# The first loads of x and wk as halves from two queues, k's first products by blocks, and one warm-up less

## The chip, the cores and the metric

The kernel runs on one core of one Trainium2 chip. The metric is the device time of one execution in microseconds (us). The kernel before takes 182.62 us, the median of 3 runs (182.56 to 182.65).

## What is computed

Two linear-attention blocks A and B work on the same input x (2048 rows, 640 columns, bf16), each with weights of its own, and a gate mixes their outputs row by row. Cut to what matters:

```python
def block(x, wqkv, wo):                      # x: 2048 x 640, 32 heads of 20
    q, k, v = split_heads(x @ wqkv)
    phi = lambda t: where(t > 0, t + 1, exp(t)) + 1e-6
    pq, pk = phi(q), phi(k)
    kv = einsum("hsd,hse->hde", pk, v)
    z = pk.sum(over s)
    o = einsum("hqd,hde->hqe", pq, kv) / (einsum("hqd,hd->hq", pq, z) + 1e-6)
    return merge_heads(o) @ wo

g = sigmoid((x * gate_w).sum(-1))            # one number for a row
out = g * block(x, A_wqkv, A_wo) + (1 - g) * block(x, B_wqkv, B_wo)
```

## The kernel before

x is cut into 16 chunks of 128 rows (`ST`), its 640 columns into 5 blocks of 128 (`DT`), and a row of k into two halves of 320 (`HF`, `hf` 0 and 1). TensorE (PE) contracts over partitions, so it needs x with its columns on the partitions: the tile xT. The tile xn holds x as it lies in memory. wk, wq and wv are the thirds of wqkv, each as 5 blocks of 128 rows.

The stages are: k of block A for all chunks, with q of A between them (to about 49 us); sums over the rows for A; then k, q and sums for B; then the outputs. The change touches only the start, up to the end of k of chunks 0 and 1, and the queue of loads behind it.

DMAs are issued by two engines, SP (`nc.sync`) and ACT (`nc.scalar`). Each issues its DMAs in the order of the code, and one that must wait holds up all behind it on that engine. A DMA reports its end on a semaphore. These are the first DMAs before the change:

- lines 127 and 128: chunk 0 of x from SP, chunk 1 from ACT, whole rows of 1280 bytes;
- lines 129 to 132: the five blocks of wk in turn from SP, ACT, SP, ACT, SP; the row of gate weights (`grow`, in the tile R) from ACT between ACT's two;
- lines 133 and 134: chunks 2 and 3 of x from SP by transposing DMAs, straight into xT;
- lines 136 and 137: wq in three pieces (blocks 0 and 1, 2 and 3, 4) from SP;
- lines 138 and 139: the other three quarters of xT by transposing DMAs from SP.

Meanwhile PE runs warm-ups (lines 164 and 165): products of ones with ones, six of 512 columns and one of 256, into a bank that is overwritten later. Then comes `k_first` (lines 234 to 269), whose order is written out by hand (`manual_schedule`, line 719). `turn(i)` transposes chunk i on PE, block by block (line 239). `keep(i, lo, hi)` lets VectorE (DVE) copy blocks lo to hi of it to xT (line 243). `part(cs, hfs, chunks)` issues the k products of the named blocks, halves and chunks (line 218). `gate_column` turns the gate's row on PE (line 169) and copies it into an extra column of wk (line 170), so that the second half of each k product (321 columns) also gives the gate's logit; every product of that half waits for it. `k_done` (line 223) is phi of the finished chunk: exp on ACT, the rest on DVE. Then `k_first` does chunks 2 and 3 (line 269) with xT from the transposing DMAs, and q of the first quarter follows (lines 291 and 301).

Before the change the order on PE is: turn 0, turn 1; block 0 and 1 of chunk 0 (first halves); block 0 of chunk 1; the gate's row; block 1 of chunk 1; block 2 of chunk 0; second halves of blocks 0 and 1 of chunk 0; and so on to block 2; then blocks 3 and 4 of chunk 0, of chunk 1. DVE copies blocks 0 and 1 of chunk 0, then of chunk 1, then blocks 2 to 4 of chunk 0, the gate's column, blocks 2 to 4 of chunk 1.

Of the kernel before, what the change touches and what calls it, by code (L numbers as in the profile page):

```python
# [8 lines left out]
P = 128  # L9
# [5 lines left out]
S, D, H = 2048, 640, 32  # L15
Dh = D // H
DT = D // P
ST = S // P
NB = 4
CB = 4  # L20
HB = 512
HF = D // 2
# [10 lines left out]
def kernel(  # L33
# [11 lines left out]
    nc = tc.nc  # L45
    x2 = A_x.flatten_outer_dims()
# [24 lines left out]
    xn = persist.tile([P, ST, D], BF16, name="xn")  # L71
# [34 lines left out]
    wq_dram = [A_wqkv.rearrange("(c p) f -> p c f", p=P), B_wqkv.rearrange("(c p) f -> p c f", p=P)]  # L106
# [6 lines left out]
    wk = [None, None]  # L113
    wv = [None, None]
    wq = [None, None]
    wk[0] = wpool.tile([P, DT, D + 16], BF16, tag="wk", name="wkA")
    def load_x(eng, i):
        eng.dma_start(out=xn[:, i, :], in_=x2[i * P:(i + 1) * P, :])

    def x_turned(lo, hi):  # L120
        nc.sync.dma_start_transpose(out=xT[:, :, lo:hi], in_=x2[lo:hi, :])

    def load_wk(eng, lo, hi):
        eng.dma_start(out=wk[0][:, lo:hi, 0:D], in_=wq_dram[0][:, lo:hi, D:2 * D])

    grow = R[0][0:DT, 0:P]
    load_x(nc.sync, 0)
    load_x(nc.scalar, 1)
    for c, eng in enumerate((nc.sync, nc.scalar, nc.sync, nc.scalar, nc.sync)):
        load_wk(eng, c, c + 1)  # L130
        if c == 1:
            nc.scalar.dma_start(out=grow, in_=gate_w.rearrange("(c p) -> c p", p=P))
    for i in (2, 3):
        x_turned(i * P, (i + 1) * P)
    wq[0] = wpool.tile([P, DT, D], BF16, tag="wq", name="wqA")
    for lo, hi in ((0, 2), (2, 4), (4, DT)):
        nc.sync.dma_start(out=wq[0][:, lo:hi, :], in_=wq_dram[0][:, lo:hi, 0:D])
    for n in range(1, NB):
        x_turned(n * HB, (n + 1) * HB)


    make_identity(nc, ident[:])
    for r in range(2):
        nc.gpsimd.memset(maskE[r][:], 1.0)
        for sign, base in ((1, 0), (-1, Dh - 1)):
            nc.gpsimd.affine_select(
                out=maskE[r][:], in_=maskE[r][:], pattern=[[-sign * Dh, WT[0] // Dh], [0, Dh]],
# [4 lines left out]
    for sign, base in ((1, 0), (-1, TW - 1)):  # L152
        nc.gpsimd.affine_select(
            out=headE[:], in_=headE[:], pattern=[[-sign * TW, H]],
# [6 lines left out]
    turned = [ps_raw("xt", i) for i in range(2)]  # L161
    warm = turned[1].bitcast(FP32).rearrange("p (b n) -> p b n", b=2)
    one_l, one_r = [nc.const_aps.tensor(1.0, [P, n], BF16) for n in (P, HB)]
    for n in (HB,) * 6 + (HB // 2,):
        nc.tensor.matmul(warm[:, 1, 0:n], lhsT=one_l, rhs=one_r[:, 0:n], start=True, stop=True)  # L165

    def gate_column(gcol):

        nc.tensor.transpose(out=gcol, in_=grow, identity=ident[0:DT, 0:DT])
        nc.vector.tensor_copy(out=wk[0][:, :, D:D + 1], in_=gcol.rearrange("p (c n) -> p c n", n=1))  # L170
# [45 lines left out]
    def k_mm(b, i, c, pt, hf):  # L216
        w = HF + (hf if b == 0 else 0)
        nc.tensor.matmul(  # L218
            pt[:, hf, 0:w], lhsT=xT[:, c, i * P:(i + 1) * P], rhs=wk[b][:, c, hf * HF:hf * HF + w],
            start=(c == 0), stop=(c == DT - 1),  # L220
        )

    def k_done(b, i, pt, lifted=False):
        side = (lambda: nc.scalar.copy(out=logit[:, i:i + 1], in_=pt[:, 1, HF:HF + 1])) if b == 0 else None
        phi(pk[:, i, :].rearrange("p (b n) -> p b n", b=2), pt[:, :, 0:HF], HF, lifted, side)

    def k_chunk(b, i, slot=None, lifted=False):
        pt = ps(f"k{'AB'[b]}", slot)
        for hf in range(2):
            for c in range(DT):  # L230
                k_mm(b, i, c, pt, hf)
        k_done(b, i, pt, lifted)

    def k_first():

        def turn(i):
            for c in range(DT):
                cols = slice(c * P, (c + 1) * P)
                nc.tensor.transpose(out=turned[i][:, cols], in_=xn[:, i, cols], identity=ident[:])

        def keep(i, lo, hi):
            src = turned[i][:, 0:D].rearrange("p (c n) -> p c n", c=DT)
            nc.vector.tensor_copy(out=xT[:, lo:hi, i * P:(i + 1) * P], in_=src[:, lo:hi])  # L243

        def part(cs, hfs, chunks=(0, 1)):
            for c in cs:
                for hf in hfs:
                    for i in chunks:
                        k_mm(0, i, c, pts[i], hf)

        for i in range(2):
            turn(i)
            keep(i, 0, 2)
        part((0, 1), (0,), (0,))
        part((0,), (0,), (1,))
        keep(0, 2, DT)
        gate_column(turned[1][:, 2 * HB:2 * HB + DT])
        keep(1, 2, DT)
        part((1,), (0,), (1,))
        part((2,), (0,), (0,))  # L260
        part((0, 1), (1,), (0,))
        part((2,), (0,), (1,))
        part((0, 1), (1,), (1,))
        part((2,), (1,))
        for i in range(2):
            part((3, 4), (0, 1), (i,))
            k_done(0, i, pts[i])
        for i in range(2, CB):
            k_chunk(0, i, i - 2)
# [278 lines left out]
    part = [slice(n * RB, (n + 1) * RB) for n in range(4)]  # L548
# [170 lines left out]
    with tc.manual_schedule():  # L719
        k_first()  # L720
# [19 lines left out]
    with tc.manual_schedule():  # L740
# [100 lines left out]
        for i in range(half - 1):  # L841
            p, after = pairs[i:i + 2]
# [48 lines left out]
```

## Time and profile before

| | before |
|---|---|
| median of 3 runs | 182.62 us (182.56 to 182.65) |
| the profiled execution's own time | 182.69 us |
| its span, first to last instruction | 180.9 us |
| PE busy | 177.1 us (98%), 1340 matmuls |
| DVE busy | 147.5 us (81%) |
| ACT busy | 85.8 us (47%) |
| granted clock of TensorE | 1.00 |

The profile is that of one execution. Its times count from the first instruction of the span. "PE" are matmuls, "PEld" the weight loads ahead of them, "SPq" and "ACTq" the DMA issues of SP and ACT. A matmul's recorded length holds its way through the array, so the pace of a row of matmuls is read from their starts. "Landing" is the time from a DMA's issue to its end; a row has one only where the trace could tell it. Behind `<-` in square brackets stands what ended the engine's idle time.

### The profile page before, as it was taken

The numbers are of one execution on the slowest core, as the hardware profiler recorded it, in microseconds if no ns is written. First come the engines' busy times: TensorE is split into PE (matmuls) and PEld (weight loads), VectorE is DVE, ScalarE is ACT, GpSimd is POOL, SyncE is SP. The second block draws the span as 40 slices with busy tenths as digits, with TensorE's granted clock in tenths as the row PEclk, the third lists the DMA queues.
The fourth block names the chain that finished last, engine by engine and source line by source line (L and its number), as shares of the span: only waits on it lengthen the run. The fifth ranks groups of instructions, "written<-read, shape, count | busy, mean of one in ns | idle before, by whom it ended". The sixth has DMA issues, their size and how long they took to land.

```text
span 180.9 us, 3414 instructions
## 1 busy us (share of the span) xinstructions
PE 177.1 (98%) x1340; PEld 119.3 (66%) x1345; DVE 147.5 (81%) x247; ACT 85.8 (47%) x140; POOL 5.4 (3%) x18
## 2 busy tenths in 40 slices
PE   8999999999999999999999999999999999999993
PEld 4566657765577777777775555677777777677772
DVE  0386868989998896888778999969999799977863
ACT  2245846889971101378784779921101863111010
POOL 6000000000000000000000000000003200000000
PEclk9999999999999999999999999999999999999999
DMA  5999999523100216431116000000325451133323
GB/s 179 209 269 173 244 370 284 112 49 134 58 0 6 70 47 209 110 108 36 57 34 190 19 0 0 0 4 14 125 78 132 137 181 50 36 109 112 109 92 127
DMA packets 22842, 19.33 MB, mean 107 GB/s; under 512 B 10538, under 2 KB 22058, under 8 KB 22826
## 3 DMA queue, kind: packets, MB, share of 16 engines
q1 hardware_dynamic: 20744, 16.95, 34.0%
q10 hardware_dynamic: 2082, 2.17, 3.6%
q8 instruction: 10, 0.16, 0.4%
q14 instruction: 6, 0.05, 0.1%
HBM read 12.29 MB, written 4.53 MB: 93 GB/s over the span
## 4 chain that ended last, share of the span: by engine, by line
PE 97%; issue 0%; DVE 0%
PE gs L370 17%; PE kA L218 12%; PE ox L590 12%; PE kB L218 12%; PE qB L281 12%; PE qA L281 6%; PE oz L590 6%; PE qA L291 5%; PE gB L329 2%; PE gA L329 2%; PE ow L590 2%; PE xt L165 2%; PE qA L301 1%; PE mA L494 1%; PE s L494 1%; PE oy L590 1%
## 5 line engine op out<-in xcount | busy, mean ns | idle before, releaser
L218 PEld LDWEIGHTS <-xT 128*128 128x128 bf16 x320 | 31.0, 98 | 12.8 <-DVE xT L243 0.2
L210 DVE TENSOR_SCALAR e<-e 128x640 bf16<-128x640 bf16 (+2 forms) x53 | 18.9, 357 | 7.3 <-ACT e L205 6.7
L218 PE MATMUL kB<-wkB,xT 128*128 128x320 bf16 x160 | 23.1, 299 | 0.0
L218 PE MATMUL kA<-wkA,xT 128*128 128x320 bf16 (+1 forms) x160 | 22.9, 301 | 0.0
L281 PE MATMUL qB<-xT,wqB 128*128 128x512 bf16 x98 | 21.6, 379 | 0.1
L205 ACT ACTIVATE e<-kB 128x640 bf16<-128x640 f32 x16 | 11.2, 703 | 15.8 <-DMA wqB<-in_B_wqkv_dram 9.4
L281 PEld LDWEIGHTS <-wqB 128*128 128x128 bf16 x100 | 11.7, 117 | 9.7
L205 ACT ACTIVATE e<-kA 128x640 bf16<-128x640 f32 x16 | 11.2, 704 | 8.3 <-PE kA L218 8.3
L205 ACT ACTIVATE e<-qA 128x1024 bf16<-128x1024 f32 (+1 forms) x11 | 10.4, 946 | 6.4 <-PE qA L291 5.1
L648 ACT COPY u<-ox 128x320 f32<-128x320 f32 x8 | 3.4, 425 | 20.6 <-PE ox L590 20.6
L205 ACT ACTIVATE e<-qB 128x1024 bf16<-128x1024 f32 x10 | 10.2, 1023 | 5.6 <-PE qB L281 4.9
L370 PEld LDWEIGHTS <-xn 128*128 128x128 bf16 x96 | 9.2, 98 | 3.9 <-issue 0.4
L370 PEld LDWEIGHTS <-S 128*128 128x128 bf16 x96 | 9.4, 98 | 3.6
L281 PE MATMUL qA<-xT,wqA 128*128 128x512 bf16 x49 | 10.9, 379 | 0.1
L214 DVE SCALAR_TENSOR_TENSOR pk<-kB,e 128x640 bf16<-128x640 f32 x12 | 9.9, 824 | 1.2
L590 PEld LDWEIGHTS <-xT 128*128 128x128 bf16 x85 | 8.1, 98 | 2.9
L590 PEld LDWEIGHTS <-pqTB 128*128 128x128 bf16 x80 | 7.8, 98 | 3.3 <-issue 0.2
L590 PEld LDWEIGHTS <-pqTA 128*128 128x128 bf16 x80 | 7.7, 98 | 2.9
L370 PE MATMUL gs<-pk,xn 128*128 128x320 bf16 x64 | 9.5, 299 | 0.0
L281 PEld LDWEIGHTS <-wqA 128*128 128x128 bf16 x50 | 5.9, 117 | 4.8
L291 PE MATMUL qA<-xT,wqA 128*128 128x512 bf16 x38 | 8.9, 379 | 0.1
L212 DVE TENSOR_TENSOR pk<-pk,e 128x640 bf16<-128x640 bf16 x12 | 5.9, 492 | 2.8 <-ACT pk L209 2.2
(123 smaller groups left out, 296.9 us busy)
## 6 DMA issues: line engine op xcount, KB each, us to landing
xn<-in_A_x_dram SPq DMA_DIRECT2D x1, 2240.0 KB, 10.0
out_dram<-pk SPq DMA_DIRECT2D x14, 160.0 KB, 1.8
wvA<-in_A_wqkv_dram SPq DMA_DIRECT2D x1, 800.0 KB
wkB<-in_B_wqkv_dram SPq DMA_DIRECT2D x1, 800.0 KB, 4.7
wqB<-in_B_wqkv_dram ACTq DMA_DIRECT2D x1, 800.0 KB, 6.5
wvB<-in_B_wqkv_dram SPq DMA_DIRECT2D x1, 800.0 KB
MA<-mA_dram SPq DMA_DIRECT2D x1, 800.0 KB, 6.1
MB<-mB_dram SPq DMA_DIRECT2D x1, 800.0 KB
```

The costliest lines, as they stand in the source:

```text
L165: nc.tensor.matmul(warm[:, 1, 0:n], lhsT=one_l, rhs=one_r[:, 0:n], start=True, stop=True)
L205: nc.scalar.activation(out=e[:], in_=src, func=ACT.Exp)
L210: nc.vector.tensor_scalar(e[:], e[:], 1.0, EPS, op0=ALU.min, op1=ALU.add)
L212: nc.vector.tensor_tensor(out=dst, in0=dst, in1=e[:], op=ALU.max)
L214: nc.vector.scalar_tensor_tensor(out=dst, in0=src, scalar=1.0 + EPS, in1=e[:], op0=ALU.add, op1=ALU.max)
L218: nc.tensor.matmul(pt[:, hf, 0:w], lhsT=xT[:, c, i * P:(i + 1) * P], rhs=wk[b][:, c, hf * HF:hf * HF + w], start=(c == 0), stop=(c == DT - 1),
L281: nc.tensor.matmul(pt[:, u, :], lhsT=mixed(wq[b][:, c, :], m), rhs=xT[:, c, n * HB:(n + 1) * HB], start=(c == 0), stop=(c == DT - 1),)
L291: nc.tensor.matmul(pt[:, u, :], lhsT=mixed(wq[b][:, c, :], m + u), rhs=xT[:, c, n * HB:(n + 1) * HB], start=(c == 0), stop=(c == DT - 1),)
L329: nc.tensor.matmul(pt[:, hf, 0:HF], lhsT=xn[:, i, c * P:(c + 1) * P], rhs=pk[:, i, hf * HF:(hf + 1) * HF], start=(i == 0), stop=(i == ST - 1),
L370: nc.tensor.matmul(pt[:, n, 0:HF], lhsT=left[:, i, n * P:(n + 1) * P], rhs=right[:, i, :], start=(first and i == 0), stop=(i == hc - 1), s ...
L494: nc.tensor.matmul(dst[:w, 0:HF], lhsT=KVA[:rows, k, 0:w], rhs=wo_sb[b][:rows, k, n * HF:(n + 1) * HF], start=True, stop=True,)
L590: nc.tensor.matmul(dst, lhsT=left[:, c, r0:r0 + P], rhs=right[:, c, :], start=(first and c == 0), stop=(c == DT - 1), skip_group_check=not ...
```

## The change

- Chunks 0 and 1 of x and block 0 of wk come one after the other, each as two DMAs: its first 320 columns from SP, its last 320 from ACT.
- Then SP issues block 1 of wk and ACT the gate's row, ACT block 2, and SP blocks 3 and 4 in one DMA.
- wq comes in two pieces (blocks 0 to 2, blocks 3 and 4) instead of three, and the last two quarters of xT in one transposing DMA instead of two. The number of DMAs ahead of xn's rest stays 16.
- One of the six warm-ups of 512 columns is left out.
- DVE copies all of chunk 0 before chunk 1's first blocks, and the k products go by blocks: block 0 of both chunks, the gate's row, block 1 of both chunks, the second halves of blocks 0 and 1, then block 2.

```diff
-    def load_x(eng, i):
-        eng.dma_start(out=xn[:, i, :], in_=x2[i * P:(i + 1) * P, :])
+    sides = [(nc.sync, slice(0, HF)), (nc.scalar, slice(HF, D))]
+
+    def load_x(i):
+        for eng, cols in sides:
+            eng.dma_start(out=xn[:, i, cols], in_=x2[i * P:(i + 1) * P, cols])
...
-    load_x(nc.sync, 0)
-    load_x(nc.scalar, 1)
-    for c, eng in enumerate((nc.sync, nc.scalar, nc.sync, nc.scalar, nc.sync)):
-        load_wk(eng, c, c + 1)
-        if c == 1:
-            nc.scalar.dma_start(out=grow, in_=gate_w.rearrange("(c p) -> c p", p=P))
+    for i in range(2):
+        load_x(i)
+    for eng, cols in sides:
+        eng.dma_start(out=wk[0][:, 0, cols], in_=wq_dram[0][:, 0, D + cols.start:D + cols.stop])
+    load_wk(nc.sync, 1, 2)
+    nc.scalar.dma_start(out=grow, in_=gate_w.rearrange("(c p) -> c p", p=P))
+    load_wk(nc.scalar, 2, 3)
+    load_wk(nc.sync, 3, DT)
     for i in (2, 3):
         x_turned(i * P, (i + 1) * P)
     wq[0] = wpool.tile([P, DT, D], BF16, tag="wq", name="wqA")
-    for lo, hi in ((0, 2), (2, 4), (4, DT)):
+    for lo, hi in ((0, 3), (3, DT)):
         nc.sync.dma_start(out=wq[0][:, lo:hi, :], in_=wq_dram[0][:, lo:hi, 0:D])
-    for n in range(1, NB):
-        x_turned(n * HB, (n + 1) * HB)
+    for lo, hi in ((1, 2), (2, NB)):
+        x_turned(lo * HB, hi * HB)
...
-    for n in (HB,) * 6 + (HB // 2,):
+    for n in (HB,) * 5 + (HB // 2,):
...
         for i in range(2):
             turn(i)
             keep(i, 0, 2)
-        part((0, 1), (0,), (0,))
-        part((0,), (0,), (1,))
-        keep(0, 2, DT)
+            if i == 0:
+                keep(0, 2, DT)
+        part((0,), (0,))
         gate_column(turned[1][:, 2 * HB:2 * HB + DT])
         keep(1, 2, DT)
-        part((1,), (0,), (1,))
-        part((2,), (0,), (0,))
-        part((0, 1), (1,), (0,))
-        part((2,), (0,), (1,))
-        part((0, 1), (1,), (1,))
-        part((2,), (1,))
+        part((1,), (0,))
+        part((0, 1), (1,))
+        part((2,), (0, 1))
         for i in range(2):
             part((3, 4), (0, 1), (i,))
             k_done(0, i, pts[i])
```

## The prediction

> **What bounds the kernel now.** I read the page's shares first, then its chain.
>
> ```profile
> PE 177.1 (98%) x1340; PEld 119.3 (66%) x1345; DVE 147.5 (81%) x247; ACT 85.8 (47%) x140; POOL 5.4 (3%) x18
> PE 97%; issue 0%; DVE 0%
> ```
>
> PE works for 177.1 of 180.9 us and is 97% of the chain that ended last. So time can only be won where PE idles, or where it does work that nobody needs. All the edits lie in the first loads and in k's first products, so next comes the chain's first stretch, in order of time (start, length, what).
>
> ```profile
> 0.83 2.93 PE xt L165 x7
> 3.77 1.07 PE xt L239 x10
> ...
> 4.86 0.80 PE kA L218 x3
> ...
> 5.77 5.31 PE kA L218 x37
> ```
>
> The reader is to see two things. First, 2.93 us of L165 are the warm-ups, filler that runs until x is there. Second, TensorE is slow at first: three k products take 0.80 us (0.27 each), the next 37 take 5.31 (0.14 each, with a wait among them). The timeline of the head has the warm-ups too at the slow pace, 0.43 for 512 columns (2.50 and 2.92), which at 0.14 for 320 would be 0.22:
>
> ```profile
> 0.79 0.41 ACTq L118 DMA_DIRECT2D xn<-in_A_x_dram  x1
> 0.80 0.39 SPq L118 DMA_DIRECT2D xn<-in_A_x_dram  x1
> 1.23 0.46 ACTq L124 DMA_DIRECT2D wkA<-in_A_wqkv_dram  x1
> 1.25 1.37 SPq L124 DMA_DIRECT2D wkA<-in_A_wqkv_dram  x3
> 1.72 0.58 ACTq L132 DMA_DIRECT2D R<-in_gate_w_dram  x1
> 2.33 0.36 ACTq L124 DMA_DIRECT2D wkA<-in_A_wqkv_dram  x1
> 2.50 0.15 PEld L165 LDWEIGHTS <-const-bfloat16-1.0 128*128 128x128 bf16 x1 [0.28 <-issue]
> 2.73 1.28 ACT L205 ACT_TABLE_LOAD   x1 [2.73 <-issue]
> 2.92 0.15 PEld L165 LDWEIGHTS <-const-bfloat16-1.0 128*128 128x128 bf16 x1 [0.28 <-issue]
> 3.58 0.98 PEld L239 LDWEIGHTS <-xn 128*128 128x128 bf16 x10 [0.51 <-DMA xn<-in_A_x_dram]
> 3.59 1.25 PE L239 MATMUL xt<-ident,xn 128*128 128x128 bf16 x10
> 3.73 2.64 SPq L121 DMA_TRANSPOSE xT<-in_A_x_dram  x2
> 4.34 0.29 DVE L243 COPY xT<-xt 128x256 bf16<-128x256 bf16 x1 [3.37 <-PE xt L239]
> 4.87 0.55 DVE L243 COPY xT<-xt 128x256 bf16<-128x256 bf16 x2 [0.24 <-PE xt L239]
> ...
> 6.41 1.60 SPq L137 DMA_DIRECT2D wqA<-in_A_wqkv_dram  x3
> ```
>
> So full speed comes at about 5.4, some 4.5 us after the first matmul at 0.83. The turning of x starts at 3.59, where the last warm-up (half of one, from 3.35) ends and where x chunk 0 has just landed: warm-ups and x end together. Five instants of narrow timelines close the head: the first product of chunk 1, the last one of block 2, the first ones of block 3 and of chunk 2, and q's first.
>
> ```profile
> 5.35 0.31 PE L218 MATMUL kA<-wkA,xT 128*128 128x320 bf16 x1
> 6.86 0.30 PE L218 MATMUL kA<-wkA,xT 128*128 128x321 bf16 x1
> 7.10 0.43 PE L218 MATMUL kA<-wkA,xT 128*128 128x320 bf16 x2
> 8.19 0.43 PE L218 MATMUL kA<-wkA,xT 128*128 128x320 bf16 x2
> 10.91 0.38 PE L291 MATMUL qA<-xT,wqA 128*128 128x512 bf16 x1
> ```
>
> From 8.19 on PE runs without a gap worth counting, so **the change is worth what it moves the start of chunk 2, 8.19**, as long as later loads keep up.
>
> **The change part by part.**
>
> *One warm-up less.* It takes one interval, 2.92 - 2.50 = 0.42 to 0.43 us: filler ends at 3.16 instead of 3.59. This is a gain only if x is there; if not, PE idles instead and nothing is won.
>
> *x in halves, one chunk after the other.* Landings (the last number, median us from the issue) come from the DMA view, rates from windows, whose last column is GB/s:
>
> ```profile
> wqA<-in_A_wqkv_dram SPq DMA_DIRECT2D x2, 320.0 KB, 3.6
> wkA<-in_A_wqkv_dram SPq DMA_DIRECT2D x3, 160.0 KB, 3.6
> wkA<-in_A_wqkv_dram ACTq DMA_DIRECT2D x2, 160.0 KB, 3.8
> xn<-in_A_x_dram ACTq DMA_DIRECT2D x1, 160.0 KB, 2.9
> ...
> xT<-in_A_x_dram SPq DMA_TRANSPOSE x3, 3.9
> ```
>
> ```profile
> 1.50:1.75 0.25, 0.25 (x2) 0.11 (x1) 0.00 (x0) 0.00 (x0) 0.25 (x1) 1.00 0.00 0
> 1.75:2.64 0.89, 0.89 (x4) 0.33 (x3) 0.00 (x0) 0.00 (x0) 0.85 (x6) 1.00 0.78 184
> 1.75:3.08 1.33, 1.33 (x5) 0.48 (x4) 0.00 (x0) 0.35 (x1) 1.29 (x8) 1.00 0.86 247
> 1.75:3.53 1.78, 1.78 (x6) 0.48 (x4) 0.00 (x0) 0.81 (x1) 1.62 (x9) 1.00 0.92 278
> ```
>
> A chunk of x is 164 kB. 0.89 x 184 = 164 kB are moved by 2.64, 1.33 x 247 = 328 kB (both chunks) by 3.08, 1.78 x 278 = 495 kB (and one block of wk) by 3.53. Chunk 1, issued at 0.79, landed at 0.79 + 2.9 = 3.69, which is 0.61 after the bytes for both were through. Today chunk 0 shares the engines with chunk 1; after the change its halves have them alone, so chunk 0 should land near 2.64 + 0.61 = 3.25. Rows of 640 bytes cost more per byte. The queue rows of two windows (2.75 to 3.5 with 1280-byte reads; 177.55 to 177.95 with mostly 640-byte stores) price them:
>
> ```profile
> DMA packets 252, 0.28 MB, mean 374 GB/s; under 512 B 33, under 2 KB 252, under 8 KB 252
> ...
> q1 hardware_dynamic: 146, 0.17, 65.7%
> q10 hardware_dynamic: 106, 0.12, 42.5%
> ```
>
> ```profile
> q10 hardware_dynamic: 137, 0.08, 62.1%
> ```
>
> 252 packets took 108.2% of 16 x 0.75 us, 51.5 ns each; 137 took 62.1% of 16 x 0.40, 29 ns each. Two halves are 58 against 51.5, or 12%: 0.1 us on 0.89. I take 3.35 for chunk 0 (bounds: 3.16, where the filler ends and nothing earlier helps, and 3.69, where chunk 1 lands today). [...]
>
> The transposes go by columns of 128, and the first two need the left half alone, so only the third (0.21 later) waits for the right half. The chain then behaves as if turning began at about 3.20 (bounds 3.16 and 3.55).
>
> *Products by blocks.* Today the first product of chunk 1 comes 5.35 - 3.59 = 1.76 after the first transpose: five transposes, DVE's copy of chunk 0, five transposes, DVE's copy of chunk 1. The new order puts the copy of chunk 0's last three blocks ahead of chunk 1's first copy; DVE idles 0.24 there now (4.63 to 4.87), and the copy is about 0.3, so I charge nothing (bounds: -0.03 and +0.1). That product comes at 3.20 + 1.76 = 4.96. Its wk block, as two halves, is third in line: 3.53 + 0.61 plus 0.2 for small rows, 4.35, before the first product at about 4.45 (the row's 3.6 from 1.25 is 4.85 today).
>
> From there to chunk 2 takes 2.84 today, which holds 0.11 of waiting for block 3 (6.86 + 0.136 = 6.99, it starts at 7.10). The new order has one product more behind this point (18, not 17; +0.14), does not wait there (-0.11), and runs about 0.08 of it at half speed, since full speed comes at 5.4 and does not move with x. 4.96 + 2.84 + 0.14 - 0.11 + 0.08 = 7.91, against 8.19: **-0.28 us**.
>
> *What is issued later.* The transposing DMA at 3.73 writes a part of xT that nothing has touched, and still the queue's waits say:
>
> ```profile
> SPq L121 <- DMA xn<-in_A_x_dram: 1.1, 1, 1.1
> ```
>
> It is the ninth DMA, it leaves when chunk 1 has landed (3.69), so eight may be under way, and the ninth waits for the first. After the change eight DMAs are x (four), wk block 0 (two), block 1 and the gate's row. **The ninth and tenth are wk block 2 and blocks 3 to 4.** Today these leave by about 2.6 (L124's rows); then they leave when chunk 0's halves have landed, about 3.35. First bytes follow an issue by 1.0 us (issue 0.80, nothing moves before 1.75), so at 4.35; the engines are then just done with block 1 (3.53 + 164 kB at 374 GB/s + 0.2 for small rows = 4.2). 492 kB at 374 GB/s are 1.3 us: through at 5.7, landed at 6.3 by the lag of 0.61. By the wk rows (3.6 to 3.8 from the issue) they land at 7.05. Needed: block 2 at 6.28, block 3 at 7.91 - 8 x 0.136 = 6.82. I charge nothing, near the first estimate, and keep the second for the range. Behind them in SP's queue, the transposing DMA for chunk 2 moves from 3.73 to about 3.9 (3.35 + 0.55); at 3.9 to landing that is 7.8, so chunk 2 may start at 7.9 and not before. ACT's table load (1.28) waits behind block 2's issue, and ends near 5.2; the first exp has to wait for chunk 0's last product anyway, after 6.82. wq in two pieces and xT's last two blocks as one are the same bytes from the same queue: wq's first piece leaves near 6.5 (6.41 today) and takes the row's 3.6 plus 0.4 for a block more: 10.5, needed at 10.91 - 0.28 = 10.63; nothing is charged (bound +0.2). Block 1 (SP's fourth, not ACT's second) and the gate's row (ACT's fourth, not third) leave 1.0 and 0.5 later: block 1 is through at 4.2 and landed at 4.8, needed at 5.3; the gate's row is needed at 5.2, and I charge nothing (bound +0.1).
>
> **The sum.** 182.69 (profiled execution; span 180.9 and 1.8 around it) - 0.28 = 182.41; the median of the runs lies 0.07 lower, so 182.34, rounded **182.35 us**. Own range 182.26 to 182.52. About 0.2%, 0.37 us, is what a measurement of this kernel can tell from no change.
>
> **The rivals.**
>
> *All of the warm-up is won* (0.17): the halves land by 3.2, and the transposing DMA does not bind: chunk 2 at 7.8, 182.1 to 182.25. For it: the byte count. Against it: the half-speed clock until 5.4, and 7.8 for chunk 2's xT.
>
> *The halves come no sooner* (0.13): the change doesn't do what it says. If a half on ACT's queue lands as chunk 1 does now, 3.6 to 3.69, PE idles where the warm-up was: turning as from 3.45 to 3.55, chunk 2 at 8.15 to 8.25, 182.55 to 182.7. For it: packets, not bytes, may set the slow start (184 GB/s on average until 2.64). Against it: right behind that the two queues run at 374 GB/s.
>
> *The late blocks of wk* (0.14) end on the slower side: blocks 2 to 4 wait for chunk 0's landing, and transposing DMAs crowd them. Today block 3 is issued at 2.33 and used at 7.10, 4.8 later; from 3.35 that is 8.1, 1.3 past the need of 6.82, 183.6. With half of that excess, 183.0. It is slower than before once block 3 lands after 7.06. For it: PE waits for block 3 even now. Against it: by 4.35 the engines have little else to do.
>
> *The clock* (0.08): if filler that ends early lets TensorE idle at about 3.2 to 3.4, full speed may come 4.5 us after the transposes' start, 7.7 instead of 5.4. That stretch at half speed loses 1.15 us, 183.5. Against it: three runs within 0.09 us, and idle of the same size at 4.63 to 4.86 now. [...]
>
> **How the numbers follow.** Forecast 0.48, rivals 0.17, 0.13, 0.14, 0.08. Faster by over 0.2%: 0.17. Within: 0.48 + 0.13 + 0.04 (late blocks that cost little) = 0.65. Slower: 0.10 + 0.08 = 0.18. Range 182.1 to 183.1: it leaves out the clock and the upper half of the late blocks.
>
> **What would show it.** Right: six L165 matmuls, the first transpose at about 3.2, the first product of chunk 1 near 4.95, no gap ahead of blocks 2 and 3, chunk 2 near 7.9, q's first product near 10.6 instead of 10.91. Wrong: a PE idle of 0.3 or more ahead of L239 (halves), a gap ahead of block 2 or 3 with SP's or ACT's queue waiting for xn at L124 (late blocks), k products of 0.27 after 5.5 (clock).

## The result and the profile after

The changed kernel takes 183.87 us, the median of 22 runs (182.98 to 185.76), against 182.67 for the kernel before in the same sessions (22 runs, 182.19 to 185.19). It is slower by 1.2 us. The ratio of the mean times is 1.008, with an interval of 1.0061 to 1.0098; it leaves out three executions in a slow state (two of before, one of the change), so it is not quite that of the medians. The forecast was 182.35, its range 182.1 to 183.1; what came is the rival "late blocks of wk", and a little more than its 183.0 to 183.6.

The profiled execution took 183.81 us, with a span of 182.1 against 180.9. Its page has these two lines in the place of those shown of before:

```profile
PE 176.5 (97%) x1339; PEld 119.0 (65%) x1344; DVE 147.3 (81%) x247; ACT 85.8 (47%) x140; POOL 5.4 (3%) x18
PE 94%; DMA 4%; issue 0%; DVE 0%
```

TensorE does 0.6 us less work, of which one warm-up is 0.4, and still the span is 1.2 longer: idle time has come in. The chain now has 4% of DMA where it had none. The timeline of TensorE in the head says where (start, length, what; in brackets the idle time ahead and what ended it):

```profile
0.84 2.51 PE L170 MATMUL xt<-const-bfloat16-1.0 128*128 128x512 bf16 x6 [0.84 <-PEq L877]
3.14 0.74 PE L244 MATMUL xt<-ident,xn 128*128 128x128 bf16 x5
4.05 0.54 PE L244 MATMUL xt<-ident,xn 128*128 128x128 bf16 x5 [0.18 <-DMA xn<-in_A_x_dram]
4.80 0.50 PE L223 MATMUL kA<-wkA,xT 128*128 128x320 bf16 x2 [0.20 <-DMA wkA<-in_A_wqkv_dram]
5.23 0.17 PE L174 MATMUL xt<-ident,R 5*128 5x5 bf16 x1
5.33 1.04 PE L223 MATMUL kA<-wkA,xT 128*128 128x320 bf16 x6
7.73 4.52 PE L223 MATMUL kA<-wkA,xT 128*128 128x320 bf16 x32 [1.35 <-DMA wkA<-in_A_wqkv_dram]
12.08 2.11 PE L293 MATMUL qA<-xT,wqA 128*128 128x512 bf16 x8
```

The head starts as forecast: chunk 0 is turned from 3.14. The products of blocks 0 and 1 run from 4.80 to about 6.4. Then TensorE stands for 1.35 us, until block 2 of wk is there. The first product of q comes at 12.08 against 10.91, 1.17 later, and that is the whole loss in this execution: from q on both kernels take 170.0 us (182.1 - 12.08, 180.9 - 10.91). The chain of the head, in order of time, leads back from the products of block 2:

```profile
0.80 2.37 DMA xn<-in_A_x_dram
3.17 0.02 issue
3.19 4.50 DMA wkA<-in_A_wqkv_dram
7.68 0.04 issue
7.73 4.52 PE kA L223 x32
```

Block 2 was issued at 3.19, 0.02 after the last half of chunk 0 had landed, and took 4.50 us. The waits of the issuing engines name the same releaser (us in total, times, longest):

```profile
ACT L210 <- DMA xn<-in_A_x_dram: 3.6, 1, 3.6
SPq L124 <- DMA xn<-in_A_x_dram: 0.8, 1, 0.8
SPq L127 <- DMA xn<-in_A_x_dram: 0.4, 1, 0.4
```

L127 is the load of blocks 3 and 4, L124 the first transposing load, and L210, ACT's first instruction behind the issue of block 2, stands for that issue. None of the three loads touches xn. Block 2 is the ninth load, blocks 3 and 4 the tenth, the transposing load the eleventh, and they wait for the first three: they are issued at 3.19, 3.03 and 4.23, each 0.02 behind the landing of a half of chunk 0 or 1 (3.17, 3.01 and 4.21 by their semaphores' events).

**The account.** Before, block 3 was the last to be waited for (7.10), and behind it stood the eight products of blocks 3 and 4; chunk 2 began at 8.19. Now blocks 2, 3 and 4 land at the same time, 7.68 (block 2 by the chain, 3 and 4 by their semaphore's events), TensorE goes on at 7.73, and twelve products stand behind that. So 0.63 us are the later landing (7.73 - 7.10), 0.54 are block 2's four products of 0.136 that could be done ahead of the last landing before and cannot now. The sum is 1.17.

### The profile page after: what moved, and what is told of

The parts are those of the page before. It is cut to its first block, busy times and chain, and to the rows that moved or that the text cites. A ratio compares the mean times of both kernels' runs of the same rounds, so it can differ in the third digit from the quotient of the medians.

```text
span 182.1 us, 3411 instructions
## 1 busy us (share of the span) xinstructions
PE 176.5 (97%) x1339; PEld 119.0 (65%) x1344; DVE 147.3 (81%) x247; ACT 85.8 (47%) x140; POOL 5.4 (3%) x18
## 3 DMA queue, kind: packets, MB, share of 16 engines
q10 hardware_dynamic: 2226, 2.09, 3.7%
## 4 chain that ended last, share of the span: by engine, by line
PE 94%; DMA 4%; issue 0%; DVE 0%
PE gs L372 17%; PE ox L592 12%; PE kB L223 12%; PE qB L283 12%; PE kA L223 11%; PE qA L283 6%; PE oz L592 6%; PE qA L293 5%; DMA wkA<-in_A_wqkv_dram 2%; PE gB L331 2%; PE gA L331 2%; PE ow L592 2%; DMA xn<-in_A_x_dram 1%; PE qA L303 1%; PE mA L496 1%; PE s L496 1%
## 5 line engine op out<-in xcount | busy, mean ns | idle before, releaser
L210 ACT ACTIVATE e<-kB 128x640 bf16<-128x640 f32 x16 | 11.3, 703 | 15.8 <-DMA wqB<-in_B_wqkv_dram 9.4
L210 ACT ACTIVATE e<-kA 128x640 bf16<-128x640 f32 x16 | 11.2, 704 | 8.6 <-PE kA L223 8.6
L210 ACT ACTIVATE e<-qA 128x1024 bf16<-128x1024 f32 (+1 forms) x11 | 10.4, 946 | 6.4 <-PE qA L293 5.1
L210 ACT ACTIVATE e<-qB 128x1024 bf16<-128x1024 f32 x10 | 10.2, 1023 | 5.6 <-PE qB L283 4.9
```

Source lines behind the costliest of these rows:

```text
L210: nc.scalar.activation(out=e[:], in_=src, func=ACT.Exp)
```

## The experiments

The ratios are to runs of the kernel before on the same chip, with 95% intervals. Kernels built on the changed one carry its later loads, its order of products and its 5.5 warm-ups, where nothing else is said.

**The parts that seemed harmless.** e3 is the kernel before with one warm-up less:

```diff
-    for n in (HB,) * 6 + (HB // 2,):
+    for n in (HB,) * 5 + (HB // 2,):
```

> The kernel before with one warm-up less and nothing else. Both theories: x chunk 0 lands at 3.54 as before, PE idles 0.4 ahead of the first transpose, the same time as before within 0.1 (182.6 to 182.75). If the full clock came later for the missing work, 1 us more.

Measured: 182.58 us (12 runs), ratio 1.0012 (0.9987 to 1.0037). TensorE idles 0.38 us ahead of the turning instead. e4 is the kernel before with only the new order in `k_first` (the last hunk of the change):

```diff
         turn(i)
         keep(i, 0, 2)
+            if i == 0:
+                keep(0, 2, DT)
-        part((0, 1), (0,), (0,))
...
+        part((0,), (0,))
...
+        part((2,), (0, 1))
```

> The kernel before with the new order of DVE's copies and of k's products and nothing else. Both theories: block 1 and block 2 are needed at nearly the same times as before, block 3 still ends the wait, the same time within 0.15. If the order by blocks needs its loads earlier than they come, 0.2 to 0.4 more.

Measured: 182.66 us (12 runs), ratio 0.9994 (0.9985 to 1.0003). Neither median shows any of the loss, though two of e3's twelve runs took 184.55 and 184.73.

**First theories: late issue, small rows, crowding.** e1 keeps the halves and has no large load behind the eighth; the gate's row is ninth:

```diff
-    load_wk(nc.sync, 1, 2)
+    load_wk(nc.sync, 1, 3)
+    load_wk(nc.scalar, 3, DT)
     nc.scalar.dma_start(out=grow, in_=gate_w.rearrange("(c p) -> c p", p=P))
-    load_wk(nc.scalar, 2, 3)
-    load_wk(nc.sync, 3, DT)
```

> The changed kernel, but the eight DMAs ahead are x (four), wk block 0 (two), blocks 1 and 2 in one from SP, blocks 3 and 4 in one from ACT; only the gate's row is ninth. All halves of 640 bytes stay. Theory (late issue: the ninth DMA waits for the first): no large load waits, the 1.35 us idle ahead of block 2 shrinks to 0.3 or less, 182.5 to 182.9. Rival (small rows make every load behind them slow): blocks 1 to 4 still land past 7, a gap of 0.8 or more stays ahead of some block, 183.4 or more.

Measured: 187.17 us (5 runs), ratio 1.0247 (1.0225 to 1.027). The timeline of TensorE shows that the last wait is for the ninth load, though it is 1.2 KB: issued at 3.16, it is there at 8.5.

```profile
8.53 0.18 PE L173 MATMUL xt<-ident,R 5*128 5x5 bf16 x1 [2.67 <-DMA R<-in_gate_w_dram]
```

Of the two loads of two blocks each, issued at 2.2, SP's landed 5.9 us later, at 8.1, so TensorE would have waited until 8.1 even with the gate's row in time: no load of wk was held, and still the forecast of 182.5 to 182.9 failed. That looked like a price of small rows. e2 tests it: halves of 64 rows of 1280 bytes instead of 128 of 640, everything else as in the change.

```diff
-    sides = [(nc.sync, slice(0, HF)), (nc.scalar, slice(HF, D))]
+    sides = [(nc.sync, slice(0, P // 2)), (nc.scalar, slice(P // 2, P))]
...
-            eng.dma_start(out=xn[:, i, cols], in_=x2[i * P:(i + 1) * P, cols])
+            eng.dma_start(out=xn[rows, i, :], in_=x2[i * P + rows.start:i * P + rows.stop, :])
```

> The changed kernel with halves by rows (64 rows of 1280 bytes each) instead of by columns: as many DMAs in the same order, but no 640-byte rows. Theory (late issue): blocks 2 to 4 still leave only when chunk 0 has landed, at 3.1 to 3.4, and the gap ahead of block 2 stays at 1 us or more, 183.5 to 184.0. Rival (small rows): the loads move at 350 GB/s or more from 3.1 on, block 2 lands by 6.5, 182.5 to 183.0.

Measured: 184.29 us (6 runs), ratio 1.0088 (1.0058 to 1.0119): the whole loss without one small row. Block 2 was issued at 3.76 and its products began at 8.01. But only 0.34 us of TensorE's waiting lie ahead of block 2, where I had expected 1 or more; 1.04 lie ahead of block 0, which is late here too. e5 is the change with the first two transposing loads moved behind wq:

```diff
-    for i in (2, 3):
-        x_turned(i * P, (i + 1) * P)
     wq[0] = wpool.tile([P, DT, D], BF16, tag="wq", name="wqA")
     for lo, hi in ((0, 3), (3, DT)):
         nc.sync.dma_start(out=wq[0][:, lo:hi, :], in_=wq_dram[0][:, lo:hi, 0:D])
+    for i in (2, 3):
+        x_turned(i * P, (i + 1) * P)
```

> The changed kernel with the two transposing DMAs (chunks 2 and 3) moved behind wq in SP's queue; blocks 2 to 4 of wk are still ninth and tenth and leave at 3.0 to 3.2 as in the changed kernel. If the late issue alone makes them late, block 2's products still start at 7.3 to 7.7. If the transposing DMAs crowd out what shares the engines with them, blocks 2 to 4 land by 6.3, the 1.35 us idle ahead of block 2 goes (0.2 or less), and PE idles ahead of chunk 2 instead; the total time, 183 to 185, says nothing here.

Measured: 185.27 us (2 runs), ratio 1.0137 (1.0104 to 1.017). In the timeline of its TensorE block 2, issued at 3.16, still keeps TensorE waiting, and chunk 2 now waits for its xT:

```profile
7.26 1.79 PE L223 MATMUL kA<-wkA,xT 128*128 128x320 bf16 x12 [0.50 <-DMA wkA<-in_A_wqkv_dram]
10.65 2.90 PE L223 MATMUL kA<-wkA,xT 128*128 128x320 bf16 x20 [1.60 <-DMA xT<-in_A_x_dram]
```

Block 2 takes 4.1 us here instead of 4.5, so the transposing loads are not needed to make it late. What crowding costs is not shown by this: wq, 800 KB, is issued from 3.74 in their place and shares the stretch with block 2.

**Some halves undone, eight loads, nothing late.** e6 halves only chunk 0, e8 only block 0; e7 has no halves.

```diff
     # e6
-    for i in range(2):
-        load_x(i)
-    for eng, cols in sides:
-        eng.dma_start(out=wk[0][:, 0, cols], in_=wq_dram[0][:, 0, D + cols.start:D + cols.stop])
-    load_wk(nc.sync, 1, 2)
-    nc.scalar.dma_start(out=grow, in_=gate_w.rearrange("(c p) -> c p", p=P))
-    load_wk(nc.scalar, 2, 3)
+    load_x(0)
+    nc.scalar.dma_start(out=xn[:, 1, :], in_=x2[P:2 * P, :])
+    load_wk(nc.sync, 0, 1)
+    load_wk(nc.scalar, 1, 2)
+    load_wk(nc.sync, 2, 3)
+    nc.scalar.dma_start(out=grow, in_=gate_w.rearrange("(c p) -> c p", p=P))
     load_wk(nc.sync, 3, DT)
```

> Only chunk 0 of x in halves; chunk 1 whole from ACT, blocks 0 and 2 whole from SP, block 1 from ACT, the gate's row from ACT, blocks 3 and 4 from SP: eight DMAs, so no load of wk waits for x; five and a half warm-ups and the new order of products. Late issue alone: chunk 0 lands by 3.2, blocks 2 to 4 by 6.5, chunk 2 starts at 7.9, 182.3 to 182.5. Crowding: the transposing DMA, ninth, leaves as soon as chunk 0's half has landed, 3.2 instead of 3.73, and blocks 3 and 4 land at 7.1 or later, 182.6 to 183.2.

```diff
     # e7; in e8 only the first of the two loops is replaced
-    for i in range(2):
-        load_x(i)
-    for eng, cols in sides:
-        eng.dma_start(out=wk[0][:, 0, cols], in_=wq_dram[0][:, 0, D + cols.start:D + cols.stop])
+    for i, eng in enumerate((nc.sync, nc.scalar)):
+        eng.dma_start(out=xn[:, i, :], in_=x2[i * P:(i + 1) * P, :])
+    load_wk(nc.sync, 0, 1)
```

> The changed kernel with all three halvings undone (chunk 0 and block 0 whole from SP, chunk 1 whole from ACT), the rest as changed. Seven DMAs, so nothing large waits and no small rows: by the late issue and by the small rows as causes alike, 182.5 to 182.8. But the first transposing DMA is eighth, waits for nothing and leaves near 2.8: if transposing DMAs crowd out the loads under way, blocks 1 to 4 land at 7 or later and the time is 183.5 or more.

> Only wk block 0 in halves; chunks 0 and 1 whole as before the change, the rest as changed. Eight DMAs, nothing of wk waits, the first transposing DMA leaves when a chunk of x has landed (3.5 to 3.7), as before the change. Late issue and crowding: 182.5 to 182.8. Small rows as the cause: block 0's 256 rows alone cost 0.3 to 0.5, 183.0 to 183.2.

Measured: 184.61 (ratio 1.009, 1.0056 to 1.0123), 184.74 (1.0111, 1.0083 to 1.0139) and 184.59 (1.0109, 1.0076 to 1.0142), 6 runs each. No theory had that: TensorE waits for no block of wk in e6 and e7, and both are as slow as the change. The timelines show products that take 0.175 and 0.19 us each on the mean of their stretch instead of 0.14. First e6, then e7:

```profile
6.24 6.66 PE L222 MATMUL kA<-wkA,xT 128*128 128x320 bf16 x38
```

```profile
6.06 7.25 PE L222 MATMUL kA<-wkA,xT 128*128 128x320 bf16 x38
```

Their TensorE idles ahead of the turning (0.62 us ahead of chunk 1 in e6, 0.59 ahead of chunk 0 in e7), and full speed comes only at 9.0 and 10.0 instead of 5.4: windows of 1 us hold 5 or 6 matmuls from 6.0 up to there, 9 or 10 behind it.

The execution profiled of e8 (183.72, the lowest of its six) is another case: block 2 waits for no other load to land, leaves at 2.34, and still TensorE waits for it, 0.17 us.

```profile
2.34 4.72 DMA wkA<-in_A_wqkv_dram
7.06 0.04 issue
7.11 1.26 PE kA L223 x8
```

So 4.5 us is no more than a block of wk takes in this stretch without being held: 4.72 here, and block 3 of the kernel before left at 2.33 and was used at 7.10. The change adds the later start, 3.19 instead of 2.33 for the load that ends the wait.

**The pace.** The expectations call the half pace the clock. In the windows of e6 and e7 the granted clock reads 1.00 all the while, so the runs show the pace and not that it is a clock. e9 is e6 with products of ones in its gaps (three of 256 columns ahead of chunk 1's turning, two ahead of the gate's row); e10 is e7 with 7.5 warm-ups; e12 is the change with one product of 256 columns between the turnings and six of 512 ahead of block 2. These fillers compute nothing that is used.

```diff
     # e9, behind the first chunk's keep; e12 likewise with other counts
+                for _ in range(3):
+                    nc.tensor.matmul(warm[:, 1, 0:256], lhsT=one_l, rhs=one_r[:, 0:256], start=True, stop=True)
...
     # e10
-    for n in (HB,) * 5 + (HB // 2,):
+    for n in (HB,) * 7 + (HB // 2,):
```

> Only chunk 0 of x comes in halves, eight loads as in e6_x0_halved_only, and the idle time that e6 had is filled with products of ones: three of 256 columns between the transposes of chunks 0 and 1, two of 256 ahead of the gate's row. The clock theory (e6 lost its time because TensorE idled .62 and .42 us in the head and its clock opened at 8.95 instead of about 5): full clock by about 5.5, time near 182.4 (182.0 to 182.9), about 2 us under e6. The late-blocks theory and the small-rows theory give e6's loads no fault (block 2 was in at 5.69), so they have no price for e6 and none here; if this kernel still takes 184 or more, the clock was not what e6 lost.

> All loads whole, as in e7_all_whole, with two more full warm-ups (7.5 instead of 5.5), so that TensorE works until chunk 0 of x is in at 3.9. The clock theory: full clock by about 5.5 instead of 9.97, which takes some 4.4 us at half speed away, about 2 us: 182.5 to 183.0. If the crowding by the early transposing load (issued 2.66) is what e7 pays for: 184 or more, as e7.

> The changed kernel, with its waits filled by products of ones: one of 256 columns between the transposes of chunks 0 and 1, six of 512 ahead of block 2. Late blocks alone: the products hide in the waits, the time stays at 183.6 to 184.0. If the clock has a share in the changed kernel's median and spread (182.98 to 185.76): the runs above 184.3 go away and the median falls to 183.4 to 183.7, but not to the kernel before's 182.7.

Measured: e9 183.65 us (6 runs, ratio 1.005, 1.0032 to 1.0067), e10 183.96 (9 runs, 1.006, 1.0037 to 1.0083), e12 184.23 (6 runs, 1.0098, 1.0066 to 1.0129). The first product groups after the gate's row, e9's and e10's:

```profile
6.18 5.40 PE L222 MATMUL kA<-wkA,xT 128*128 128x320 bf16 x38
```

```profile
6.83 5.34 PE L222 MATMUL kA<-wkA,xT 128*128 128x320 bf16 x38 [0.77 <-DMA wkA<-in_A_wqkv_dram]
```

With the filler the pace is 0.14 us a product from 6.18 and 6.83 on, and the medians fall by 1.0 and 0.8, half of what I expected. So by the medians what the filler takes away is between a third and a half of e6's and e7's loss; the intervals overlap (e6 and e9) or touch (e7 and e10). In e12 the filler bought nothing: 184.23 is not below the change's 183.87, and two of the six runs stay above 184.3. The execution profiled is the slowest of the six (186.01): block 0 came at 5.62 there, the products ran at half pace until the filler (0.26 us each from 6.36), and the filler's six products took 2.14 us and held up block 2. That the half pace has no share in the change's median is therefore not shown.

**Late or small?** e11 is e10 with the gate's row in four small loads. Block 2 is the ninth load again, blocks 3 and 4 the tenth, with the waits of the change, but all rows are whole.

```diff
-    nc.scalar.dma_start(out=grow, in_=gate_w.rearrange("(c p) -> c p", p=P))
+    for c, eng in enumerate((nc.scalar, nc.sync, nc.scalar, nc.scalar)):
+        hi = (1, 2, 3, DT)[c]
+        eng.dma_start(out=grow[c:hi, :], in_=gate_w.rearrange("(c p) -> c p", p=P)[c:hi])
```

> As e10, all rows whole, but the gate's row comes as four small loads, so that block 2 of wk is again the ninth load and blocks 3 and 4 the tenth, with the waits that the changed kernel has (for the first and the second load, here whole chunks of x at 3.9 and 4.1). Late issue alone as the cause: block 2 is issued at about 3.9, lands about 4.5 later at 8.3, TensorE idles about 2 us ahead of it, time 184.0 to 184.8 with the clock in order. Small rows as the cause: with whole rows a late load takes no more than about 2.5 us, so block 2 lands by 6.5 and the time is at most .3 above e10's.

Measured: 183.9 us (6 runs), ratio 1.007 (1.0051 to 1.0088). The chain of its head:

```profile
0.80 3.13 DMA xn<-in_A_x_dram
3.93 0.02 issue
3.96 3.85 DMA wkA<-in_A_wqkv_dram
7.81 0.04 issue
7.85 4.52 PE kA L224 x32
```

It is the chain of the change without halves. Chunk 0 lands 0.76 later (3.93 against 3.17), block 2 takes 0.65 less, and TensorE goes on 0.12 later. So small rows are not needed for such a wait. The time does not price it, though: e11 is within 0.1 of e10 (183.96), which has block 2 in time. There I had expected 184.0 to 184.8 from the late issue and at most 0.3 above e10 from the small rows. In its execution profiled e10 waits for another block, 0.77 us at 6.83, and later for MB, which is told below. e17 and e18 take the other side: nothing late, the order, warm-ups and later loads of before, two loads of two blocks each. e17 has x in halves; e18 has it whole, and the gate's row in three small loads.

```diff
     # e17, in the place of the loads from block 0 on; e18 has the same loads of wk
+    load_wk(nc.sync, 0, 1)
+    nc.scalar.dma_start(out=grow, in_=gate_w.rearrange("(c p) -> c p", p=P))
+    load_wk(nc.sync, 1, 3)
+    load_wk(nc.scalar, 3, DT)
```

> The kernel before with chunks 0 and 1 of x in halves and the number of loads kept at eight: block 0 whole, blocks 1 and 2 in one load, 3 and 4 in one. Nothing is late (blocks 1 and 2 are issued at 2.2 or so, as in the kernel before), the order of the products, the warm-ups and the later loads are those of before, so that four small-row loads are all that differs from e18. If the wait for chunk 0 is what held the blocks in the changed kernel: blocks 1 to 4 in by 6.5, 182.5 to 183.0, and within .3 of e18. If the 640-byte rows slow everything behind them: blocks 1 to 4 at 7.0 to 8.0, 183.2 to 185, and .5 or more above e18.

> The twin of e17 with both chunks of x whole and the gate's row in three small loads to make eight. Both theories: blocks 1 to 4 in by 6.5, 182.6 to 183.1. If it is slower than that (183.3 or more), merging blocks 1 and 2 costs by itself, and e17 has to be read against this kernel and not against the one before.

Measured: 186.44 us (4 runs, ratio 1.0204, 1.0183 to 1.0226) and 186.41 (6 runs, 1.0209, 1.0186 to 1.0233). The twins are equal, so halving x has no price that shows here; both wait for the same blocks, which could hide one. And both miss what every theory said, by 3.5 us. TensorE's timeline has the wait for block 1, first e17's, then e18's:

```profile
7.27 0.43 PE L221 MATMUL kA<-wkA,xT 128*128 128x320 bf16 x2 [1.45 <-DMA wkA<-in_A_wqkv_dram]
```

```profile
7.34 0.69 PE L219 MATMUL kA<-wkA,xT 128*128 128x320 bf16 x2 [2.45 <-DMA wkA<-in_A_wqkv_dram]
```

And SP's timeline, with the issue of that load, again e17 (the second of the two issues) and e18:

```profile
1.72 0.90 SPq L127 DMA_DIRECT2D wkA<-in_A_wqkv_dram  x2
```

```profile
2.09 0.41 SPq L124 DMA_DIRECT2D wkA<-in_A_wqkv_dram  x1
```

Blocks 1 and 2, in one load and issued in time, come 5.0 to 5.2 us later, and TensorE waits for no block behind them. That is what e1's load of two blocks had shown (5.9 us), and what I had put on small rows: block 1 was there for its product only when the load that it shares had landed. Then the granted clock falls to 0.50, which is told in the last section.

**The remaining parts.** e13 is the kernel before with only the change's later loads (wq in two, the last transposing loads in two); e14 with only its first loads (the diff's lines from `load_x` to the load of blocks 3 and 4).

```diff
     # e13
-    for lo, hi in ((0, 2), (2, 4), (4, DT)):
+    for lo, hi in ((0, 3), (3, DT)):
...
-    for n in range(1, NB):
-        x_turned(n * HB, (n + 1) * HB)
+    for lo, hi in ((1, 2), (2, NB)):
+        x_turned(lo * HB, hi * HB)
```

> The kernel before, with only the later loads of the change: wq in two loads instead of three, the transposing loads of groups 1 to 3 in two instead of three. If the head of the queues is the whole cause: 182.5 to 182.8, no difference, since these loads are issued behind 5 us and q waits for none of them. If the later loads have a share in what e10_whole_filled lost without any half and without a late block: 183.2 or more.

> The kernel before with only the change's loads of x and wk (halves, blocks 3 and 4 in one): wq, the later transposing loads, the order of the products and the warm-ups as before. If the head of the queues is the whole cause: 183.6 to 184.1, as the changed kernel, with block 2 in TensorE's way at about 7.7. If the later loads carry a part of it: 182.9 to 183.4.

Measured: e13 183.45 us (7 runs, ratio 1.0045, 1.0026 to 1.0064), e14 186.03 (6 runs, 1.0162, 1.0124 to 1.0201). The head of e13 is 0.09 later (q at 11.00); most of the rest of its loss lies 140 us further on, at the last stage's load of MB. The chain of before there has TensorE alone, that of e13 has the load:

```profile
149.38 1.36 PE oz L590 x10
150.74 1.36 PE ow L590 x10
```

```profile
146.13 5.46 DMA MB<-mB_dram
151.59 0.04 issue
151.63 1.52 PE ow L590 x10
```

That load arrives just in time in the kernel before: it landed at 150.53 by its semaphore's events, and its first product starts at 150.58. In e13 it landed at 151.59, and TensorE waited 0.77 us. e10 (0.63), e17 (0.4) and e8 (0.2) wait there too; the change does not. e14's chain has the late block, later still:

```profile
0.80 2.40 DMA xn<-in_A_x_dram
3.20 0.02 issue
3.22 5.11 DMA wkA<-in_A_wqkv_dram
8.32 0.04 issue
8.37 6.74 PE kA L223 x36
```

So the first loads alone carry the loss, and more than all of it. The new order leaves less undone at the wait (32 products against 36), so it should help beside late blocks; no run shows that by itself.

e15 merges blocks 3 and 4 in the kernel before and nothing else, which moves the first transposing load forward to the eighth place; e16 also splits the gate's row in two, so that it is the ninth again.

```diff
-    for c, eng in enumerate((nc.sync, nc.scalar, nc.sync, nc.scalar, nc.sync)):
-        load_wk(eng, c, c + 1)
+    for c, eng in enumerate((nc.sync, nc.scalar, nc.sync, nc.scalar)):
+        load_wk(eng, c, (c + 1, DT)[c == 3])
```

```diff
     # e16, in addition
-            nc.scalar.dma_start(out=grow, in_=gate_w.rearrange("(c p) -> c p", p=P))
+            for eng, lo, hi in ((nc.scalar, 0, 2), (nc.sync, 2, DT)):
+                eng.dma_start(out=grow[lo:hi, :], in_=gate_w.rearrange("(c p) -> c p", p=P)[lo:hi])
```

> The kernel before with blocks 3 and 4 of wk in one load and nothing else changed: seven loads and the gate's row are then eight less one, so the first transposing load is the eighth and is issued at about 2.7, beside x and the first blocks, not at 3.7. If an early transposing load takes the head's bandwidth (the cause of e10's and e7's times): chunk 0 at about 3.9, block 1 at 6 to 6.8, 183.4 to 184.2. If the merged load or the early transposing load costs nothing: 182.5 to 182.9.

> As e15, and the gate's row in two small loads, so that the first transposing load is the ninth again and waits for chunk 0 of x, as in the kernel before. If the early transposing load is what e15 pays for: 182.5 to 182.9, as before. If the merged load of blocks 3 and 4 is: as e15.

Measured: 182.72 us (11 runs, ratio 1.0007, 0.9998 to 1.0016) and 183.02 (11 runs, 1.0017, 1.0007 to 1.0026). Merging the last two blocks, with block 2 in a load of its own and not held, is no cause, or one of 0.3 us at most (e16); nor is an early transposing load. No version is faster than the kernel before by more than the noise.

Block 2 of wk over these kernels, from the rows above and the timelines:

| kernel | halves | block 2 issued, why | its products begin | median |
|---|---|---|---|---|
| before | none | not held | before 6.86, the last of them | 182.67 |
| e15 | none | 1.72, not held | 6.38 | 182.72 |
| e8 | columns, block 0 alone | 2.34, not held | 7.11 | 184.59 |
| the change | columns | 3.19, ninth | 7.73 | 183.87 |
| e11 | none | 3.96, ninth | 7.85 | 183.9 |
| e2 | rows | 3.76, ninth, 0.04 behind ACT's issue of the gate's row | 8.01 | 184.29 |
| e14 | columns | 3.22, ninth | 8.37 | 186.03 |
| e18 | none | 2.09, in one load with block 1 | behind 7.34 | 186.41 |

e6, e7, e9 and e10 are left out: their block 2 is not held, and yet they take 183.65 to 184.74. No run took the late issue alone out of the change and came back to 182.67. That the ninth load waits, and what it costs in the execution profiled, the chain shows; that the whole difference of the medians is its price is argued from there.

## Why the prediction was wrong, step by step

- **One warm-up less, halves of x: right.** Turning was forecast from 3.20 and came at 3.14; chunk 0 landed at 3.17 where I had taken 3.35.
- **Products by blocks: right in the number, in part by luck.** The first product of chunk 1 was forecast for 4.96. It is the second of the two from 4.80, and starts at 4.99. But chunk 1 could be turned only from 4.05, as its halves had not landed, and the forecast had both turnings back to back; that was made up behind it, where the five transposes took 0.54 us in all, against 0.74 for the five before them. And block 0, forecast for 4.35, held its first product until 4.80.
- **The ninth and tenth load: the mechanism was right, its price was the failure.** "The ninth and tenth are wk block 2 and blocks 3 to 4", and they wait for chunk 0: so it was. The step that failed is "through at 5.7, landed at 6.3 by the lag of 0.61 ... I charge nothing, near the first estimate, and keep the second for the range". They landed at 7.68, 1.4 after the one estimate and 0.6 after the other bound, 7.05. I had worked from the best rate of a window (374 GB/s) and from engines that had nothing else to do. Moving the bytes was mis-sized, more than the lag behind them: ACT's queue, which carries block 2, still has 10 packets between 6.5 and 7.0 and none from 7.0 to 7.7, where 5.7 was forecast. The 4.8 that block 3 took before the change, which only the rival used, would have said 8.0 from 3.19; e8's block 2, not held, took 4.72. The windows of the changed kernel, the last two columns the share of the DMA engines and GB/s:

```profile
3.10:3.80 0.70, 0.70 (x7) 0.51 (x5) 0.00 (x0) 0.22 (x1) 0.31 (x2) 1.00 0.82 180
4.70:5.90 1.20, 1.10 (x7) 0.59 (x7) 0.66 (x3) 0.16 (x1) 0.00 (x0) 1.00 0.99 272
6.40:7.75 1.35, 0.02 (x1) 0.02 (x1) 0.00 (x0) 0.00 (x0) 0.00 (x0) 1.00 1.30 163
```

  The kernel before has, in the first of these windows:

```profile
3.10:3.80 0.70, 0.70 (x6) 0.22 (x4) 0.00 (x0) 0.70 (x1) 0.30 (x2) 1.00 1.06 368
```

  While the ninth load waits, less is moved: 0.70 x (368 - 180) = 132 kB, which at the later 272 GB/s is 0.5 us, about the 0.63 by which the last landing moved. That this gap is the cause of the 0.63 is argued from the sizes, not shown by an experiment of its own. Nor is it only a queue that has run low: the share of the engines fell by a quarter, the rate by half. Per share of 1.00 that is 220 GB/s now and 347 before. The change moves half rows in this window; e2, with whole rows, has 297 there:

```profile
3.10:3.80 0.70, 0.67 (x7) 0.43 (x5) 0.00 (x0) 0.00 (x0) 0.32 (x2) 1.00 0.77 229
```

- **"Needed: block 2 at 6.28, block 3 at 6.82"** was about right: the last product ahead of block 2 starts at 6.08. But no step priced the need of block 2. Both estimates gave one landing time for all three blocks, and at 7.05 block 2 would have been 0.77 late with twelve products behind it: chunk 2 at about 8.7 and 183.2, outside the own range of 182.26 to 182.52. The rival's "slower than before once block 3 lands after 7.06" counts eight products; with block 2's four behind the landing too, the limit was 6.5. They did land together, and those four products, 0.54 us, moved behind the landing.
- **Transposing loads crowd** (part of the rival): not needed, e5; their price is open. **640-byte rows** (12%, 0.1 us): chunk 0 landed 0.18 earlier than forecast with them, but the windows from 3.10 point to 35% or more for what came next (220 against 297), if the rows are all that differs there. They are not needed for the loss, as e2 and e11 have it without them; what part they have in the change's own is open. The rival, priced by block 3 alone, gave 183.0 to 183.6.
- **A bound that would have been next.** I had the transposing load of chunk 2 at 3.9, landing at 7.8. It was issued at 4.23 and landed 4.2 later, at 8.4. So chunk 2 would not have begun before 8.4 even with block 2 in time, 0.2 later than in the kernel before. wq's first piece, forecast for 10.5 and needed at 10.63, landed at 11.17 by its semaphore's events, behind the 10.91 of before. As far as this execution tells, the forecast gain was not to be had.
- **The clock** (0.08 in the prediction): not in the profiled execution, whose products run at full pace from 5.67 on at the latest (the 32 from 7.73 on in 4.52 us, 0.14 each). Three of the 22 runs have a granted clock of 0.991, and they are the slowest (185.16 to 185.76).

**What stays open:** how the 4.5 us of block 2 divide among half rows, an emptier queue and the loads issued beside it; why e13's load of MB is late, and whether that has a share in the change's median; why the change's runs spread over 2 us even at a granted clock of 1.00; and how much of e14's 2.2 us over the change is the order of products, how much the later loads and how much the granted clock.

## What to carry to other kernels

Before cutting a load in two, count the loads that may be under way: here eight (the ninth left 0.02 behind the landing of the first, at 3.19 in the change, 3.16 in e1 and 3.96 in e11), and what the ninth and tenth are decides more than what the halves bring, since each piece pushed a later load back to the landing of the first. A load that is needed next should be alone in its load and ahead of the others; bundled with another, it came 5.0 to 5.2 us after its issue in e17 and e18. Price a late load by the longest time that a load of its size takes in that stretch (4.7 here, e8), not by the best rate of a window.

## What the runs showed that I had not expected

- **Two loads from two queues landed together.** Block 2 from ACT and blocks 3 and 4 from SP landed at 7.68, though one is half as large (160 and 320 KB). From 5.0 to 6.0 SP's queue moved 135 packets and ACT's 104. Why the smaller load landed no earlier is not shown.
- **A tiny load was as slow as a large one in a busy stretch**: the gate's row, 1.2 KB, took 5.3 us in e1, and SP's load of 320 KB beside it 5.9.
- **TensorE's granted clock fell to 0.50 in e18, after a wait of about 2 us.** These windows of e18 (the column behind POOL's is the granted clock) show it idle from about 4.9 on:

```profile
5.00:6.00 1.00, 0.00 (x0) 0.00 (x0) 0.07 (x1) 0.00 (x0) 0.00 (x0) 1.00 1.03 364
6.00:7.00 1.00, 0.00 (x0) 0.00 (x0) 0.00 (x0) 0.00 (x0) 0.00 (x0) 0.99 1.26 282
7.00:8.00 1.00, 0.66 (x3) 0.14 (x2) 0.00 (x0) 0.00 (x0) 0.00 (x0) 0.50 1.11 197
8.00:9.00 1.00, 1.00 (x6) 0.63 (x6) 0.43 (x2) 0.00 (x0) 0.00 (x0) 0.50 0.93 136
9.00:10.00 1.00, 1.00 (x6) 0.53 (x5) 0.00 (x0) 0.00 (x0) 0.00 (x0) 0.50 0.95 298
10.00:11.00 1.00, 1.00 (x8) 0.64 (x7) 0.00 (x0) 0.00 (x0) 0.00 (x0) 0.80 1.07 376
```

  Read from these means it is at half from 6.99 to 10.4. TensorE works from 7.34 on, so by my estimate the loss on top of the idle time is about 1.5 us, half of the 3.06 from there to 10.4. After the 1.35 us of the change it did not fall in the execution profiled (1.00 in every window). What wait it takes is not shown. In e14 the runs part in two groups: 184.37 and 184.62 at a granted clock of 1.00, 186.0 to 186.87 at 0.991.
- **The granted clock reads 1.00 in the first microseconds, where products run at half pace** (e6 and e7 until 9.0 and 10.0, the kernel before until about 5.4): there the pace has to be read from the starts of the products, as the column does not tell it. What sets that pace is not shown: e8 idled 0.59 us ahead of its turning, as e7 did, and its 32 products from 7.11 took 0.14 each.
